# One-hot tiles of the token lists in quads of token columns

## The chip, the cores and the metric

The kernel runs on one core of a Trainium2 chip. The metric is the device time in microseconds; before the change it is 2782.22 us, the median of three runs (2782.1 to 2784.02). The engines are named as in the profile: PE is TensorE (PEld its weight loads), DVE is VectorE, ACT is ScalarE, POOL is GpSimd, SP is SyncE, which issues DMAs.

## What is computed

An attention with squared ReLU, and behind it a mixture of eight experts. Each expert takes exactly `cap` tokens; the pairs of token and expert are served in the order of their gate values. Cut to what matters:

```python
def _attn_ref(u, v, z):                       # u, v: (8, 2496, 256), z: (8, 2496, 64)
    scores = (1.0 / S) * np.matmul(z, z.transpose(0, 2, 1))
    out = np.matmul(np.maximum(scores, 0.0) ** 2, v)
    return u * out

def _moe_ref(x, w_gate, w1, w2):              # x: (19968, 256), 8 experts, F = 1024
    cap = N // E                              # 2496
    order = np.argsort(-(x @ w_gate).flatten())
    for idx in order:
        tok, e = idx // E, idx % E
        if assigned[tok] >= 0 or counts[e] >= cap:
            continue
        assigned[tok] = e
        counts[e] += 1
    for e in range(E):
        mask = assigned == e
        out[mask] = np.maximum(x[mask] @ w1[e], 0.0) @ w2[e]
    return out
```

## The kernel before

**Attention** (`attention`, up to about 1515 us) goes over 8 batches, 5 groups of 512 queries and 20 key tiles, with fp32 values split in two parts. It isn't touched.

**Tokens on the chip.** The gate values of all 19968 tokens lie as 128 partitions by J = 156 columns, padded to JP = 160. A token is a partition p and a column j; `idi` (L192 to L197) holds its number, `idh` and `idl` (L198 to L204) the number's upper part (divided by 128) and lower part (modulo 128) in bf16.

**Routing** (`route(k)`, L247) finds, eight times, the next expert that is full: a search for its threshold by histograms (L285 to L336; `hist`, L226, counts with the matmuls of L231), the tokens at the threshold (L339 to L352), which expert it is (L353 to L383), and then its list of tokens. For the list, each token of the expert gets a rank (L396 to L401). `rab` (L402 to L406) holds for each token the rank's upper part, `rab[:, 0]` (which of KT = 20 columns of the list), and its lower part, `rab[:, 1]` (which of 128 rows).

**The list** (L413 to L441) is made by matmuls, one for each token column j: the stationary operand is a one-hot tile `ob` of the row (128 slots), the moving operand `hl` holds the one-hot of the column times `idh`, and times `idl`. Summed over the 156 token columns in one PSUM tile, that puts each token's number at its place: L440 and L441 make it the integers `idx`, by which POOL gathers tokens (L450) and later writes results (L574). The columns go in four quarters of CB = 40. For each quarter DVE makes `oa` (L421: `rab[:, 0]` compared with `slot`), `hl` (L424, twice) and `ob` (L431, four pieces of 32 slots), and PE multiplies (L436). `slot` (L207) holds 0 to 127, each 40 times, and is filled by an iota on POOL. In all four tiles the 40 token columns are innermost, so that DVE's operations run along them; a matmul picks one of them, and its operands have a step of 40 elements: 128 stationary columns, and 2 x 20 = 40 moving columns. List 0 is made in two passes, of 4 and of 16 list columns (8 and 32 moving columns), which keep the same `ob` tiles.

**The experts** (L581 to L628) run in steps of (expert k, 512 tokens, 128 hidden values): `layer1` (L515, matmuls of L510 to L512, evictions L529 on ACT and L530 on DVE), `layer2` (L545, L541 to L543), transposes of gathered tokens (`turn_x`, L498 to L503), weights (`load_w`, L453, gathers on POOL; `split_w`, L464, whose L477 runs on POOL).

**Order.** `route(0)` runs first, alone. Each later `route(k)` is a generator that `advance` (L607) carries a step further twice in each step of expert k - 1, so that its instructions stand among those of the experts on DVE and PE; all of it must be done before expert k starts. A yielded number is how much of this pace a piece takes. `behind(4)` (L244) puts the instructions that make `ob` behind the L530 of four steps ago in DVE's order. The tiles `oa` and `hl` have two buffers, `ob` has four.

Of the kernel before, what the change touches and what calls it, by code (L numbers as in the profile page):

```python
# [10 lines left out]
BF = mybir.dt.bfloat16  # L11
# [3 lines left out]
OP = mybir.AluOpType  # L15
# [6 lines left out]
def tile_attention_then_moe(ctx, tc, u, v, z, w_gate, w1, w2, out):  # L22
# [36 lines left out]

    attention(tc, u, v, z, w_gate, xd, identf, made, first, 1.0 / S)  # L60
    moe(tc, xd, first, jp, identf, w1, w2, out, B, S, consts)


# [32 lines left out]
def moe(tc, xd, first, jp, identf, w1, w2, out, B, S, cp):  # L96
    nc = tc.nc
# [3 lines left out]
    KT = NT + 1  # L101
# [18 lines left out]
    with ExitStack() as ctx:  # L120
        rp = ctx.enter_context(tc.tile_pool(name="rp", bufs=1))
# [4 lines left out]
        def const(shape, dt, name):  # L126
            return cp.tile(shape, dt, name=name)
# [59 lines left out]
        for c in range(2):  # L187
            for h in range(DH):
# [6 lines left out]
                       base=0, channel_multiplier=NT)  # L195
# [8 lines left out]
        nc.vector.tensor_copy(idl, idh_i)  # L204

        CB = JP // 4
        slot = rp.tile([128, 128, CB], BF, name="slot")  # L207
        nc.gpsimd.iota(slot, pattern=[[1, 128], [0, CB]], base=0, channel_multiplier=0,  # L208
                       allow_small_or_imprecise_dtypes=True)

        asg = const([128, JP], BF, "asg")
        nc.vector.memset(asg, 0.0)
# [7 lines left out]
        def srch():  # L220
            return ps.tile([128, 512], F32, name="srch")
# [22 lines left out]
        def behind(lag):  # L244
            return tc.issue_after(paced[-lag].ins) if len(paced) >= lag else nullcontext()

        def route(k):  # L247
# [29 lines left out]
            else:  # L277
# [7 lines left out]
                for stage in range(2):  # L285
                    V = floor
                    for r, w in enumerate(widths):
                        n = (1 << w) - 1
# [6 lines left out]
                        for h in range(nh):  # L295
                            t = rp.tile([128, JP // nh, n], BF, name=f"mask{h}")
                            for a in range(0, n, 8):
                                z = min(8, n - a)
# [17 lines left out]
                        p = srch()  # L316
# [11 lines left out]
                    if stage == 0:  # L328
                        base = rp.tile([128, 1], F32, name="base")
# [16 lines left out]
                p = srch()  # L346
# [40 lines left out]
            p = srch()  # L387
# [14 lines left out]
            rab = rp.tile([128, 2, JP], BF, name="rab")  # L402
# [10 lines left out]
            obs = {}  # L413
            for a0, a1 in ((0, 4), (4, KT)) if k == 0 and KT > 4 else ((0, KT),):
                na = a1 - a0
                p = srch()
                for c in range(0, JP, CB):
                    q = slice(c, c + CB)
                    oa = rp.tile([128, KT, CB], BF, name="oa", bufs=2)[:, :na]
                    hl = rp.tile([128, 2, KT, CB], BF, name="hl", bufs=2)[:, :, :na]  # L420
                    nc.vector.tensor_tensor(oa, rab[:, 0, None, q].to_broadcast([128, na, CB]), slot[:, a0:a1],  # L421
                                            op=OP.is_equal)
                    for i, d in enumerate((idh, idl)):
                        nc.vector.tensor_mul(hl[:, i], oa, d[:, None, q].to_broadcast([128, na, CB]))  # L424
                    yield 1.5
                    if a0 == 0:
                        obs[c] = rp.tile([128, 128, CB], BF, name="ob", bufs=4)
                        for b in range(0, 128, 32):
                            z = b + 32
                            with behind(4):  # L430
                                nc.vector.tensor_tensor(obs[c][:, b:z],  # L431
                                                        rab[:, 1, None, q].to_broadcast([128, z - b, CB]),
                                                        slot[:, b:z], op=OP.is_equal)
                            yield 1.5
                    for j in range(c, min(J, c + CB)):
                        nc.tensor.matmul(p[:, :2 * na], obs[c][:, :, j - c], hl[:, :, :, j - c],  # L436
                                         start=(j == 0), stop=(j == J - 1))
                    yield
                idl_f = rp.tile([128, KT], F32, name="idl_f")[:, :na]
                nc.vector.tensor_copy(idl_f, p[:, na:2 * na])  # L440
                nc.vector.scalar_tensor_tensor(idx[:, a0:a1], p[:, :na], 128.0, idl_f, op0=OP.mult, op1=OP.add)  # L441
# [158 lines left out]
        for _ in route(0):  # L600
            pass
        N = len(seq)
        done = 0
        steps_k = {k: 0 for k in range(E)}
        gens = {k: route(k) for k in range(1, E)}

        def advance(pos):  # L607
# [340 lines left out]
```

## Time and profile before

| | |
|---|---|
| median of three runs | 2782.22 us (2782.1 to 2784.02) |
| span of the profiled execution, on its one core | 2781.9 us |
| mean granted clock of TensorE | 0.957 |
| attention | to about 1515 us |
| routing of the first expert, alone | about 1515 to 1614 us |
| experts, with the routing of the next | about 1615 to 2575 us |
| last expert | 2575 us to the end |
| list matmuls L436 | 1404: 156 with 8 moving columns, 156 with 32, 1092 with 40 |
| `ob` on DVE, L431 | 128, mean 847 ns |
| `oa` on DVE, L421, with 800 elements | 28, mean 1344 ns |
| iota of `slot` on POOL, L208 | 1, 5062 ns |

The span runs from the first to the last instruction of one profiled execution; it lies 0.3 us below the median of the runs. A row of the timeline gives the start and the duration in us, engine, line, operation, `out<-in`, shape, how many instructions are merged (x40), and in brackets how long the engine was idle before and what ended that. A row of the groups gives `busy us, mean ns | idle before, releaser`. A row of the windows gives a stretch, its length, the busy time (and instructions) of PE, PEld, DVE, ACT and POOL, then the granted clock of TensorE as a share of full speed, the busy share of the DMA engines and their GB/s; where the window is limited to one line, only the engines of this line stand there. Matmuls overlap, so the time that one takes in a stream is the distance of starts, not its duration.

### The profile page before, as it was taken

To read this page: it belongs to the slowest core of one execution; us is meant where nothing else is said; L and a number is where in the kernel's file an instruction comes from. 1 tells how busy PE (TensorE), PEld (TensorE's weight loads), DVE (VectorE), ACT (ScalarE), POOL (GpSimd) and SP (SyncE) were. 2 spreads that over 40 slices of the span, in tenths; PEclk is the share of its full clock that TensorE was granted. 3 is DMA by queue.
4 is the path that set the end of the run, shared out by engine and by line. 5 is a ranking of instruction groups with operands and counts; after the bars stand their busy time and mean duration, and the time that the engine had idled before them with its cause. 6 is when DMAs were issued, how large, how long until landed. Compare 5 with 4: busy or idle time off the path is not lost.

```text
span 2781.9 us, 51744 instructions
## 1 busy us (share of the span) xinstructions
PE 2671.3 (96%) x19733; PEld 2501.6 (90%) x19733; DVE 1996.2 (72%) x6053; ACT 1651.1 (59%) x2851; POOL 495.9 (18%) x608
## 2 busy tenths in 40 slices
PE   9999999999999999999998489999999999999998
PEld 8999999999999999999998378888888898988998
DVE  7787887787888877878877777676666767676222
ACT  8898888888888988888886022322223222323232
POOL 2000000000000000000000342434343334335341
PEclk9999999999999999999999588999999898989999
DMA  4120221210212202102000011111111111112110
GB/s 135 44 74 26 60 68 33 65 61 24 82 38 60 68 31 58 53 31 66 31 24 15 28 47 47 51 55 40 58 45 62 35 43 60 37 63 66 41 45 26
DMA packets 49417, 138.88 MB, mean 50 GB/s; under 512 B 10896, under 2 KB 18576, under 8 KB 48272
## 3 DMA queue, kind: packets, MB, share of 16 engines
q1 hardware_dynamic: 29200, 77.88, 9.2%
q0 software_dynamic: 19968, 57.70, 6.4%
q8 instruction: 154, 2.52, 0.4%
q14 instruction: 95, 0.78, 0.1%
HBM read 85.47 MB, written 40.89 MB: 45 GB/s over the span
## 4 chain that ended last, share of the span: by engine, by line
PE 89%; DVE 6%; issue 3%; POOL 1%; DMA 1%; ACT 0%; POOLq 0%; ACTq 0%; SPq 0%
PE acc L787 14%; PE acc L784 14%; PE acc L786 13%; PE sc L744 7%; PE sc L743 7%; PE y L541 5%; PE hp L510 5%; PE y L542 5%; PE y L543 5%; PE hp L511 5%; PE hp L512 4%; PE srch L436 3%; PE srch L231 2%; PE xp L498 1%; DVE oa L421 1%
## 5 line engine op out<-in xcount | busy, mean ns | idle before, releaser
L787 PE MATMUL acc<-vl,hi 128*128 128x256 f32 x3200 | 896.9, 282 | 0.0
L784 PE MATMUL acc<-vh,hi 128*128 128x256 f32 x3200 | 893.6, 281 | 0.0
L786 PE MATMUL acc<-vh,lo 128*128 128x256 f32 x3040 | 853.9, 281 | 0.0
L768 DVE TENSOR_TENSOR lo<-a,hi 128x512 fp32r<-128x512 f32 (+1 forms) x760 | 518.7, 683 | 222.2 <-ACT hi L757 207.8
L784 PEld LDWEIGHTS acc<-vh,hi 128*128 128x128 f32 x3200 | 602.1, 188 | 28.7
L787 PEld LDWEIGHTS acc<-vl,hi 128*128 128x128 f32 x3200 | 602.1, 188 | 1.7
L786 PEld LDWEIGHTS acc<-vh,lo 128*128 128x128 f32 x3040 | 571.5, 188 | 31.1
L529 ACT ACTIVATE hh<-hp 128x512 fp32r<-128x512 f32 (+1 forms) x320 | 187.1, 587 | 645.6 <-PE hp L512 575.0
L746 ACT ACTIVATE r<-sc 128x512 f32<-128x512 f32 (+1 forms) x800 | 468.8, 586 | 142.6 <-PE sc L744 137.6
L751 ACT ACTIVATE a<-r 128x512 f32<-128x512 f32 (+1 forms) x800 | 496.9, 621 | 24.4
L814 DVE SCALAR_TENSOR_TENSOR lt<-xs,wgb 128x256 bf16<-128x256 f32 x1248 | 480.0, 431 | 0.3
L541 PE MATMUL y<-w2h,hh 128*128 128x256 f32 (+1 forms) x1280 | 375.1, 293 | 0.0
L542 PE MATMUL y<-w2l,hh 128*128 128x256 f32 (+1 forms) x1280 | 369.9, 289 | 0.0
L743 PE MATMUL sc<-za 128*128 128x512 f32 (+1 forms) x800 | 316.9, 396 | 0.0
L744 PE MATMUL sc<-zb,za 128*128 128x512 f32 (+1 forms) x800 | 313.5, 392 | 0.0
L757 ACT ACTIVATE hi<-a 128x512 fp32r<-128x512 f32 (+1 forms) x480 | 298.2, 621 | 14.6
L208 POOL IOTA slot<- 128x5120 bf16 x1 | 5.1, 5062 | 1485.5 <-DVE xs L797 1485.5
L510 PE MATMUL hp<-xh,w1h 128*128 128x512 f32 (+2 forms) x646 | 269.4, 418 | 0.0
L541 PEld LDWEIGHTS y<-w2h,hh 128*128 128x128 f32 (+1 forms) x1280 | 249.9, 195 | 11.2 <-ACT hh L529 0.4
L542 PEld LDWEIGHTS y<-w2l,hh 128*128 128x128 f32 (+1 forms) x1280 | 249.5, 195 | 9.4
L511 PE MATMUL hp<-xl,w1h 128*128 128x512 f32 (+2 forms) x646 | 257.3, 398 | 0.0
L512 PE MATMUL hp<-xh,w1l 128*128 128x512 f32 (+2 forms) x646 | 255.2, 395 | 0.0
(1142 smaller groups left out, 3918.8 us busy)
## 6 DMA issues: line engine op xcount, KB each, us to landing
vr<-in_v_dram SPq DMA_DIRECT2D x32, 512.0 KB, 3.7
ur<-in_u_dram SPq DMA_DIRECT2D x32, 512.0 KB, 4.4
xd<-xs SPq DMA_DIRECT2D x32, 512.0 KB, 2.9
zb<-za SPq DMA_DIRECT2D x14, 640.0 KB, 6.7
zin<-in_z_dram SPq DMA_DIRECT2D x32, 128.0 KB, 2.1
vr<-in_v_dram SPq DMA_DIRECT2D x8, 384.0 KB, 3.2
ur<-in_u_dram SPq DMA_DIRECT2D x8, 384.0 KB, 4.5
xd<-xs SPq DMA_DIRECT2D x8, 384.0 KB, 2.3
```

What stands on the lines that cost most here:

```text
L510: nc.tensor.matmul(p[:, c], wh, xh, start=(d == 0), stop=False)
L541: nc.tensor.matmul(o, h[:, c], wh, start=first, stop=False, skip_group_check=True)
L542: nc.tensor.matmul(o, h[:, c], wl, start=False, stop=False, skip_group_check=True)
L743: nc.tensor.matmul(p, k, ZA[b][:, q], start=True, stop=False)
L744: nc.tensor.matmul(p, k, ZB[b][:, q], start=False, stop=True)
L746: nc.scalar.activation(r, p, AF.Relu, scale=scale)
L751: nc.scalar.activation(a, R.pop(n), AF.Square)
L768: nc.vector.tensor_sub(l, a, h.bitcast(F32))
L784: nc.tensor.matmul(o, h[:, c], vh, start=(kt == 0 and i % 2 == 0), stop=False, skip_group_check=True)
L786: nc.tensor.matmul(o, l[:, c], vh, start=False, stop=False, skip_group_check=True)
L787: nc.tensor.matmul(o, h[:, c], vl, start=False, stop=last, skip_group_check=True)
L814: nc.vector.scalar_tensor_tensor(t[r], XS[b, g][r, i], 1.0, WG["rows"][r, e], op0=OP.mult, op1=OP.mult, accum_out=lg[r, j, e:e + 1])
```

## The change

The 40 token columns of a quarter are cut into QN = 10 quads of QW = 4. In `oa`, `hl` and `ob` the quad comes first and the 4 columns of a quad are innermost: `[10, 20, 4]`, `[10, 2, 20, 4]` and `[10, 128, 4]` in place of `[20, 40]`, `[2, 20, 40]` and `[128, 40]`. The tiles keep their sizes. `slot` holds each number 4 times, 512 elements in place of 5120, and is read again for each quad; rows of `rab`, `idh` and `idl` are read through `by_quad`, 4 at a time, again for each slot. A matmul picks quad n and column r in it; its operands have a step of 4 elements (8 bytes) in place of 40 (80 bytes).

```diff
         CB = JP // 4
-        slot = rp.tile([128, 128, CB], BF, name="slot")
-        nc.gpsimd.iota(slot, pattern=[[1, 128], [0, CB]], base=0, channel_multiplier=0,
+        QW = 4
+        QN = CB // QW
+        slot = rp.tile([128, 128, QW], BF, name="slot")
+        nc.gpsimd.iota(slot, pattern=[[1, 128], [0, QW]], base=0, channel_multiplier=0,
                        allow_small_or_imprecise_dtypes=True)
+
+        def by_quad(row, n):
+            return row.rearrange("p (q r) -> p q r", r=QW)[:, :, None, :].to_broadcast([128, QN, n, QW])
...
-                    oa = rp.tile([128, KT, CB], BF, name="oa", bufs=2)[:, :na]
-                    hl = rp.tile([128, 2, KT, CB], BF, name="hl", bufs=2)[:, :, :na]
-                    nc.vector.tensor_tensor(oa, rab[:, 0, None, q].to_broadcast([128, na, CB]), slot[:, a0:a1],
-                                            op=OP.is_equal)
+                    oa = rp.tile([128, QN, KT, QW], BF, name="oa", bufs=2)[:, :, :na]
+                    hl = rp.tile([128, QN, 2, KT, QW], BF, name="hl", bufs=2)[:, :, :, :na]
+                    nc.vector.tensor_tensor(oa, by_quad(rab[:, 0, q], na),
+                                            slot[:, None, a0:a1].to_broadcast([128, QN, na, QW]), op=OP.is_equal)
                     for i, d in enumerate((idh, idl)):
-                        nc.vector.tensor_mul(hl[:, i], oa, d[:, None, q].to_broadcast([128, na, CB]))
+                        nc.vector.tensor_mul(hl[:, :, i], oa, by_quad(d[:, q], na))
...
-                        obs[c] = rp.tile([128, 128, CB], BF, name="ob", bufs=4)
+                        obs[c] = rp.tile([128, QN, 128, QW], BF, name="ob", bufs=4)
...
-                                nc.vector.tensor_tensor(obs[c][:, b:z],
-                                                        rab[:, 1, None, q].to_broadcast([128, z - b, CB]),
-                                                        slot[:, b:z], op=OP.is_equal)
+                                nc.vector.tensor_tensor(obs[c][:, :, b:z], by_quad(rab[:, 1, q], z - b),
+                                                        slot[:, None, b:z].to_broadcast([128, QN, z - b, QW]),
+                                                        op=OP.is_equal)
...
                     for j in range(c, min(J, c + CB)):
-                        nc.tensor.matmul(p[:, :2 * na], obs[c][:, :, j - c], hl[:, :, :, j - c],
+                        n, r = divmod(j - c, QW)
+                        nc.tensor.matmul(p[:, :2 * na], obs[c][:, n, :, r], hl[:, n, :, :, r],
                                          start=(j == 0), stop=(j == J - 1))
```

No instruction is added, removed or moved: on each engine the instructions stand in the same order as before, and only the shapes of the lines in the diff differ.

## The prediction

> **What bounds the kernel now.** I read the busy times first, then the chain of work that ended last, then the stretch in which the changed lines run.
>
> ```profile
> PE 2671.3 (96%) x19733; PEld 2501.6 (90%) x19733; DVE 1996.2 (72%) x6053; ACT 1651.1 (59%) x2851; POOL 495.9 (18%) x608
> PE 89%; DVE 6%; issue 3%; POOL 1%; DMA 1%; ACT 0%; POOLq 0%; ACTq 0%; SPq 0%
> PE acc L787 14%; PE acc L784 14%; PE acc L786 13%; PE sc L744 7%; PE sc L743 7%; PE y L541 5%; PE hp L510 5%; PE y L542 5%; PE y L543 5%; PE hp L511 5%; PE hp L512 4%; PE srch L436 3%; PE srch L231 2%; PE xp L498 1%; DVE oa L421 1%
> 1621.00:2575.00 954.00, 914.99 (x6716) 831.66 (x6716) 656.60 (x1649) 268.96 (x434) 366.81 (x333) 0.93 0.16 50
> ```
>
> TensorE (PE) is the bound: 96% busy and 89% of the chain. The list matmuls, L436, hold 3% of it. The last row is the stretch in which experts run while the next one's list is made: PE 915.0 of 954 us, VectorE (DVE) 656.6, ScalarE (ACT) 269.0, GpSimd (POOL) 366.8, granted clock 0.93. PE time saved there shortens the span unless DVE becomes late.
>
> **The list matmuls.** For each expert after the first (k from 1 to 7) 156 of them run in bursts. This is PE's timeline around the bursts of k = 1 (start, duration, count, idle before), with the clock over two of them from the windows view, limited to that line, and the group by shape:
>
> ```profile
> 1704.00 3.66 PE L436 MATMUL srch<-hl,ob 128*128 128x40 bf16 x40 [0.98 <-DVE ob L431]
> 1707.44 0.77 PE L510 MATMUL hp<-xh,w1h 128*128 128x512 f32 x1
> ...
> 1721.61 3.66 PE L436 MATMUL srch<-hl,ob 128*128 128x40 bf16 x40
> 1725.05 0.48 PE L510 MATMUL hp<-xh,w1h 128*128 128x512 f32 x1
> ...
> 1731.38 0.40 PE L512 MATMUL hp<-xh,w1l 128*128 128x512 f32 x1
> 1731.62 6.78 PE L436 MATMUL srch<-hl,ob 128*128 128x40 bf16 x76
> 1738.17 0.56 PE L541 MATMUL y<-w2h,hh 128*128 128x256 f32 x1
> 1704.00:1707.40 3.40, 3.40 (x40) 3.40 (x40) 0.50 0.00 0
> 1721.70:1725.00 3.30, 3.30 (x40) 3.30 (x40) 1.00 0.00 0
> L436 PE MATMUL srch<-hl,ob 128*128 128x40 bf16 x1092 | 98.8, 273 | 2.5 <-DVE ob L431 2.5
> ```
>
> From a burst's start to the next matmul's start are 3.44, 3.44 and 6.55 us, 86 ns for each list matmul. It is the same at a granted clock of 0.50 and of 1.00, so the array is not the limit; reading the operands is. The L512 row streams 512 fp32 columns in 0.24 us (to the next start), 0.47 ns a column; 40 columns at 86 ns are 2.15 ns each. Next the counts at the threshold (L231), whose weights have no step and whose 32 moving columns come in two runs of 16, and then the list matmuls of list 0, with 8 and with 32 columns, and a window over them.
>
> ```profile
> 1680.34 0.42 PE L231 MATMUL srch<-fmask,oh 128*128 128x32 bf16 x10
> 1680.61 0.48 PE L512 MATMUL hp<-xh,w1l 128*128 128x512 f32 x1
> ...
> 1577.38 2.64 PE L436 MATMUL srch<-hl,ob 128*128 128x8 bf16 x40 [6.01 <-DVE ob L431]
> ...
> L436 PE MATMUL srch<-hl,ob 128*128 128x8 bf16 x156 | 10.3, 206 | 8.3 <-DVE ob L431 8.3
> 1573.00:1594.00 21.00, 13.20 (x201) 12.85 (x202) 18.09 (x44) 2.38 (x2) 19.75 (x6) 0.50 0.20 59
> ...
> 1608.68 5.01 PE L436 MATMUL srch<-hl,ob 128*128 128x32 bf16 x76
> 1613.51 1.51 PE L498 MATMUL y<-identf,xg 128*128 128x128 f32 x6
> ```
>
> Ten counts take 0.27 us, 27 ns each. In list 0, with only 8 moving columns, 40 list matmuls take 2.64 us; less the 0.21 us of the last one, over 39, that is 62 ns. Eight columns at 2.15 ns would be 17, so it is the weights, read at a step of 40, that take 62 (at a granted clock of 0.50). With 32 columns it is (1613.51 - 1608.68) / 76 = 64 ns. I read this as two streams side by side, of which the slower one counts: the weights with 62 ns, 40 moving columns with 86.
>
> **What a step of 4 costs.** No row shows one. The bounds are 86 ns (any step costs the same) and 27 ns (a step of 4 costs nothing). A step of 4 bf16 elements is 8 bytes, next to the 4-byte step of the fp32 row at 0.47 ns a column, and far from 80 bytes. I take 30 ns. Saved for k from 1 to 7: 1092 x (86 - 30) = 61.2 us (0 to 64.4).
>
> [...]
>
> In list 0 the first 156 wait for DVE (0.76 us and more per burst) and what they feed waits for POOL:
>
> ```profile
> 1590.47 0.15 DVE L441 SCALAR_TENSOR_TENSOR idx<-srch,idl_f 128x4 int32<-128x4 f32 x1
> ...
> 1605.35 1.03 POOL L450 DMA_INDIRECT xg<-xd,idx  x1 [0.16 <-issue]
> ```
>
> The indices are there 14.9 us before POOL's first gather, so nothing is gained. The last 76 stand ahead of transposes on PE: 76 x (64 - 30) = 2.5 us (0 to 2.8).
>
> **The clock.** Windows right behind the second burst and behind the long one, of k = 1 and of k = 6, and behind the second burst of k = 7; the third last column is the granted clock:
>
> ```profile
> 1725.05:1731.62 6.57, 6.57 (x32) 5.44 (x30) 5.04 (x9) 1.14 (x2) 0.00 (x0) 0.74 0.01 2
> 1738.17:1745.62 7.45, 7.45 (x38) 6.86 (x37) 4.87 (x17) 0.60 (x1) 4.52 (x5) 0.67 0.22 59
> ...
> 2482.32:2487.36 5.04, 5.04 (x31) 4.09 (x30) 4.47 (x8) 1.14 (x2) 0.00 (x0) 1.00 0.00 0
> 2493.91:2501.36 7.45, 7.45 (x42) 7.04 (x41) 5.48 (x18) 0.75 (x2) 4.53 (x5) 0.77 0.20 55
> 2545.00:2548.00 3.00, 3.00 (x14) 2.81 (x14) 0.71 (x2) 0.60 (x1) 0.00 (x0) 0.53 0.00 0
> ```
>
> The clock falls though PE is never idle: a burst that mostly waits for its reads counts as little work. Duration times (1 - clock) is what the dense matmuls behind it lose: 1.7 and 2.5 us for k = 1. Over the 12 windows of k = 1 to 6 (clocks 0.74, 0.74, 0.74, 0.76, 0.77, 1.00 behind the second burst, 0.67 to 0.77 behind the long one) and the one of k = 7 the sum is 21.8 us. With 30 ns the bursts last 1.2 and 2.3 us and do more per time. I take 20 us (0 to 21.8), since a shorter burst may still cost the clock here and there. The low clock at the first burst (0.50 above) comes from a stall that stays (below). That it ends sooner behind a burst that is 2.2 us shorter is worth at most half of that, 1.1 us, or 6 us for six k; I count nothing.
>
> **DVE.** The one-hot operations keep their counts and elements; their inner rows become 4 long. L421 and L431 give the rate now; L70 re-reads a row of 8, L71 reads rows of 4 out of 8, L74 repeats one element along its row:
>
> ```profile
> 1573.84 0.24 DVE L421 TENSOR_TENSOR oa<-rab,slot 128x160 bf16<-128x160 bf16 x1
> ...
> 1728.49 0.81 DVE L431 TENSOR_TENSOR ob<-rab,slot 128x1280 bf16<-128x1280 bf16 x1
> ...
> L74 DVE TENSOR_TENSOR oh<-code,code8b 128x320 bf16<-128x320 bf16 x28 | 13.7, 489 | 0.7
> L70 DVE TENSOR_TENSOR eq<-eq,code8b 128x320 bf16<-128x320 bf16 x28 | 9.1, 324 | 0.5
> L71 DVE TENSOR_TENSOR eq<-eq 128x160 bf16<-128x160 bf16 x28 | 6.6, 235 | 0.2
> ...
> 1701.20 0.38 PE L543 MATMUL y<-w2h,hl__24588 128*128 128x256 f32 x1 [3.92 <-DVE hl__24588 L530]
> ```
>
> (0.81 - 0.24) / 1120 is 0.51 ns an element, plus 0.16 us. By that L70 would take 0.32 us and L71 0.24, and they do, so short rows and rows read again keep the rate; L74 comes to 1.03. I take 0.51, a cost of nothing. At 1.03 an L431 takes 0.67 us more. Before the first burst of each k PE already waits for DVE (3.92 us in the last row, then 0.98 at the burst), so there four L431 and an L424 would add 3.1 us, 22 us for seven k, and half of the 12 us that sixteen of them add in list 0: 28 us. That stall itself stays, since it lies ahead of the burst. At the long burst DVE is ahead: its last L431 ends at 1729.3, PE comes at 1731.62. If the 1.7 us of low clock in between go, 0.6 of this cover is left, and any more is a wait of that length.
>
> **The iota of slot**, on POOL, has 512 elements in place of 5120. It lies at the start of routing, where PE waits:
>
> ```profile
> 1516.04 5.06 POOL L208 IOTA slot<- 128x5120 bf16 x1 [1485.50 <-DVE xs L797]
> 1517.09 1.95 PE L831 MATMUL misc<-wgt,xt 128*128 128x8 f32 x16 [0.47 <-ACT xt L828]
> 1517.67 3.47 DVE L282 COPY hd<-nrow 128x15 f32<-128x15 f32 x1
> 1519.08 2.05 DVE L835 COPY lg<-misc 128x24 f32<-128x24 f32 x1
> ...
> L282 DVE COPY hd<-nrow x7: 170/170/3466, 1517.7 to 2292.8; 128x15 f32<-128x15 f32 x7
> ```
>
> L282 takes 0.17 us elsewhere and 3.47 here: it ends when the iota does. With a tenth of the elements, some 0.5 us,, the logits' copies (L835, L837) wait only for L831, which ends at 1519.04. They would be through near 1519.3, where they now are at 1521.2: 1.9 us (0 to 3.3).
>
> **Sum**: 61.2 + 2.5 + 20 + 1.9 = 85.6 us. The span of the profiled execution is 2781.9, 0.3 below the median of 2782.2. Forecast: 2697 us.
>
> **Rivals.**
> - *Half of the way.* If the price is for each stretch that a read fetches, and it holds two of the new columns, the burst runs at 86 / 2 = 43 ns: 1092 x 43 = 47 us, list 0 1.5, iota 1.9, clock 18. That is 2714.
> - *Weights stay slow.* If weights come quickly only where neighbours lie side by side, as in the 27 ns row, the 62 ns of the row with 8 columns stay and only the moving side gains: 1092 x 24 = 26 us, clock some 12, iota 1.9, so 2742. [...]
> - *The clock falls all the same*, since 43 or 30 ns is still thin work: 2717.
> - *DVE drops to 1.04 ns while PE gains*: 2697 + 28 = 2725. L70 and L71 speak against it.
> - *No change on PE*: any step costs 86 ns. Only the iota is left: 2780. Against it stands the fp32 row.
> - *Slower.* DVE drops to 1.04 ns in the L431 ahead of each first burst (+28 us) and PE stays at 86 ns: 2808. It decides as long as a list matmul takes more than 86 - (28 - 1.9) / 1.092 = 62 ns; below that PE's gain is the larger one.
>
> **How the numbers follow.** Chances: forecast 0.45, half 0.20, weights 0.10, clock 0.08, DVE with gain 0.07, no change 0.06, slower 0.04. The lower end takes all bounds (64.4 + 2.8 + 21.8 + 3.3 + 6 = 98): 2684. The upper end takes in all but the last two, 1 in 10: 2744. A measurement of this kernel tells about 0.2% (5.6 us) from no change: faster 0.90, same 0.06, slower 0.04.
>
> **What would show it.** The next start behind 40 list matmuls comes after 1.2 us, not 3.44, and after 76 after 2.3, not 6.55; at 1.7 us the half rival is right, at 2.5 the weights one. The windows behind them show a clock near 1.00. L431 stays at 0.82 us, and L282 takes 0.17. I am wrong if the interval is under 40 ns and the span hardly moves: then PE waits elsewhere, most likely for L530 behind the one-hot operations.

## The result and the profile after

The changed kernel takes 2705.08 us, the median of four runs (2703.23 to 2707.3), beside 2783.12 (2782.1 to 2786.07) for four runs of the kernel before: a ratio of 0.9724, with an interval of 0.9712 to 0.9735. The forecast was 2697. The span of the profiled execution went from 2781.9 to 2705.5 us, by 76.4. In the changed kernel's profile the lines from the diff on stand five or six higher: the list matmuls are L442 (were L436), `ob` is L436 (L431), the experts' matmuls are L516 to L518 and L547 to L549. First the page's busy times and the head of its chain:

```profile
PE 2585.9 (96%) x19733; PEld 2419.7 (89%) x19733; DVE 1998.9 (74%) x6053; ACT 1650.7 (61%) x2851; POOL 497.7 (18%) x608
PE 89%; DVE 7%; issue 2%; DMA 1%; POOL 1%; ACT 0%; POOLq 0%; ACTq 0%
```

The instructions are the same in number, and PE is 85.4 us less busy (2671.3 before) with DVE 2.7 us more. PE is still the bound, with 89% of the chain as before. Its timeline around the bursts of k = 1, as shown of before, with the row of the stall ahead of the first burst:

```profile
1697.18 0.39 PE L549 MATMUL y<-w2h,hl__24588 128*128 128x256 f32 x1 [3.92 <-DVE hl__24588 L536]
...
1699.99 1.83 PE L442 MATMUL srch<-hl,ob 128*128 128x40 bf16 x40 [1.26 <-DVE ob L436]
1701.65 0.78 PE L516 MATMUL hp<-xh,w1h 128*128 128x512 f32 x1
...
1715.26 1.80 PE L442 MATMUL srch<-hl,ob 128*128 128x40 bf16 x40
1716.90 0.47 PE L516 MATMUL hp<-xh,w1h 128*128 128x512 f32 x1
...
1721.92 3.28 PE L442 MATMUL srch<-hl,ob 128*128 128x40 bf16 x76
1725.03 0.37 PE L547 MATMUL y<-w2h,hh 128*128 128x256 f32 x1
```

From a burst's start to the next row are 1.66, 1.64 and 3.11 us (before 3.44, 3.44 and 6.55): 41 ns for a list matmul, where there were 86. The stall of 3.92 us ahead of the first burst is as it was. Next the windows behind the three bursts:

```profile
1701.65:1714.64 12.99, 12.99 (x78) 11.64 (x74) 10.91 (x19) 3.59 (x6) 4.46 (x4) 0.86 0.10 42
1716.90:1721.92 5.02, 5.02 (x33) 4.07 (x29) 4.45 (x8) 1.14 (x2) 0.00 (x0) 1.00 0.01 3
1725.03:1732.50 7.47, 7.47 (x56) 7.10 (x53) 6.97 (x22) 1.15 (x2) 4.59 (x5) 1.00 0.20 56
```

Behind the second burst and the long one the clock is 1.00 (it was 0.74 and 0.67); it is so for every k. Behind the first burst, which follows the stall, it is 0.86, where the same stretch of before has 0.83. The ledger needs one window more of each kernel, from the first list burst of k = 1 to the first of k = 7. Before:

```profile
1704.00:2525.94 821.94, 787.93 (x5749) 717.69 (x5750) 565.07 (x1417) 232.08 (x374) 314.56 (x285) 0.92 0.15 49
```

and after:

```profile
1699.99:2458.14 758.15, 721.60 (x5749) 654.43 (x5749) 568.90 (x1417) 231.79 (x374) 319.67 (x285) 0.97 0.16 53
```

Both hold the same 5749 matmuls, 936 of them list matmuls (six k of 156). The stretch is 63.8 us shorter. The list matmuls give 936 x (86 - 41) = 42.1 us of it. PE's busy time fell by 66.3, so the other matmuls, the same as before, took 24.2 us less: that is the clock, 0.92 against 0.97. PE's idle time grew from 34.0 to 36.6 us, which takes 2.5 back (below). Ahead of the stretch 4.0 us went (1704.00 to 1699.99), behind it 8.6, of which 156 x 45 ns = 7.0 are the list matmuls of k = 7.

The 4.0 us ahead are list 0 and the iota. List 0 (32 moving columns, the last 76 matmuls):

```profile
1575.36 1.49 PE L442 MATMUL srch<-hl,ob 128*128 128x8 bf16 x40 [6.01 <-DVE ob L436]
...
1606.74 2.73 PE L442 MATMUL srch<-hl,ob 128*128 128x32 bf16 x76
1609.31 0.58 PE L504 MATMUL y<-identf,xg 128*128 128x128 f32 x2
...
L442 PE MATMUL srch<-hl,ob 128*128 128x8 bf16 x156 | 5.8, 175 | 11.7 <-DVE ob L436 11.7
```

The 76 take 2.57 us instead of 4.83, 34 ns each. With 8 moving columns it is (1.49 - 0.175) / 39 = 34 ns too, 62 before. The iota and what it held, in the timeline:

```profile
1515.92 1.21 POOL L210 IOTA slot<- 128x512 bf16 x1 [1485.36 <-DVE xs L803]
1516.97 1.95 PE L837 MATMUL misc<-wgt,xt 128*128 128x8 f32 x16 [0.47 <-ACT xt L834]
1517.56 0.17 DVE L287 COPY hd<-nrow 128x15 f32<-128x15 f32 x1
1518.96 0.18 DVE L841 COPY lg<-misc 128x24 f32<-128x24 f32 x1 [1.24 <-PE misc L837]
1519.40 0.69 PE L236 MATMUL srch<-mask,oh 128*128 128x240 bf16 x5 [0.48 <-DVE lg L843]
```

L287 takes 0.17 us (3.47 before, as L282), and the logits' copy follows its matmuls. The gate matmul L837 starts at 1516.97, 2.43 us ahead of the first count; in the kernel before these are 1517.09 and 1521.41, 4.32 us. So 1.9 us went here.

The idle time that was added lies ahead of the first bursts, where PE waits for `ob`. The group row of before, in the prediction, has 2.5 us of such waits; here it is

```profile
L442 PE MATMUL srch<-hl,ob 128*128 128x40 bf16 x1092 | 48.6, 214 | 5.3 <-DVE ob L436 5.3
```

At k = 1 the burst starts 2.80 us after the end of the stall in the kernel before (1701.20 to 1704.00) and 2.81 us after it here (1697.18 to 1699.99): DVE's last `ob` sets that time. PE's ten matmuls in between got faster, so PE waits 1.26 us in place of 0.98. At k = 2 the same ten take 2.02 us at a clock of 0.65, 2.50 before at 0.50, and the wait is 0.78 in place of 0.30. So 2.5 us of what the clock gave did not shorten the span.

PE also waits in the searches, and there nothing was added: 11.2 us in this stretch before, 10.1 after. But what it waits for changed. At k = 1 it was L238 before (PE idle for 1.48 us):

```profile
1755.53 3.03 POOL L477 TENSOR_TENSOR w1l<-wr,w1h 128x512 fp32r<-128x512 f32 x2
1756.66 1.98 DVE L238 TENSOR_TENSOR hx<-hr,dE 128x56 fp32r<-128x56 f32 x1
```

and it is the mask behind L298 now (PE idle for 1.48 us again):

```profile
1742.59 3.03 POOL L483 TENSOR_TENSOR w1l<-wr,w1h 128x512 fp32r<-128x512 f32 x2
1743.12 2.53 DVE L298 TENSOR_TENSOR T<-next,Dg 128x7 int16<-128x7 f32 x1
```

L238 takes 0.22 us elsewhere (on average in the kernel after, as L243), and L298 a median of 0.17. Both end here within 0.1 us of the end of the same POOL subtraction (L477, now L483). In five of the k it holds L238 before, and L298 after.

### The profile page after: what moved, and what is told of

Same layout as the page of the kernel before. It is cut to its first block, busy times and chain, and to the rows that moved or that the text cites. A ratio compares the mean times of both kernels' runs of the same rounds, so it can differ in the third digit from the quotient of the medians.

```text
span 2705.5 us, 51744 instructions
## 1 busy us (share of the span) xinstructions
PE 2585.9 (96%) x19733; PEld 2419.7 (89%) x19733; DVE 1998.9 (74%) x6053; ACT 1650.7 (61%) x2851; POOL 497.7 (18%) x608
## 4 chain that ended last, share of the span: by engine, by line
PE 89%; DVE 7%; issue 2%; DMA 1%; POOL 1%; ACT 0%; POOLq 0%; ACTq 0%
PE acc L793 14%; PE acc L790 14%; PE acc L792 13%; PE sc L750 7%; PE sc L749 7%; PE hp L516 5%; PE y L547 5%; PE y L549 5%; PE y L548 5%; PE hp L517 5%; PE hp L518 5%; PE srch L442 2%; PE srch L236 2%; PE xp L504 1%; DVE ob L436 1%
## 5 line engine op out<-in xcount | busy, mean ns | idle before, releaser
L547 PE MATMUL y<-w2h,hh 128*128 128x256 f32 (+1 forms) x1280 | 367.9, 288 | 0.0
L548 PE MATMUL y<-w2l,hh 128*128 128x256 f32 (+1 forms) x1280 | 363.3, 284 | 0.0
L763 ACT ACTIVATE hi<-a 128x512 fp32r<-128x512 f32 (+1 forms) x480 | 298.2, 621 | 14.6
L516 PE MATMUL hp<-xh,w1h 128*128 128x512 f32 (+2 forms) x646 | 264.7, 411 | 0.1
L518 PE MATMUL hp<-xh,w1l 128*128 128x512 f32 (+2 forms) x646 | 252.2, 390 | 0.0
L547 PEld LDWEIGHTS y<-w2h,hh 128*128 128x128 f32 (+1 forms) x1280 | 242.3, 189 | 10.9 <-ACT hh L535 0.4
L548 PEld LDWEIGHTS y<-w2l,hh 128*128 128x128 f32 (+1 forms) x1280 | 242.4, 189 | 9.1
```

The source lines that it names most:

```text
L516: nc.tensor.matmul(p[:, c], wh, xh, start=(d == 0), stop=False)
L547: nc.tensor.matmul(o, h[:, c], wh, start=first, stop=False, skip_group_check=True)
L548: nc.tensor.matmul(o, h[:, c], wl, start=False, stop=False, skip_group_check=True)
```

## Experiments

The kernels ran on chips where the kernel before takes 2811.74 us (first four kernels), 2813.12 (the next four) and 2812.22 (the last two), some 29 us more than beside the result. Why was not tried; the change itself (`a_quads`) is longer there by as much between its first list burst of k = 1 and its last list matmul, 827 us against 798. The times in the expectations of the first four kernels count from the result's chip (2782 us before, 2705 with quads), so only their differences can be compared. Each is compared with the runs of before that stand beside it, or with `a_quads`, the change itself on such a chip. The list matmuls are L445 in all kernels but `a_quads`, `ob` is L439. `QO` stands for the group width of `ob`, `QH` for that of `oa` and `hl`; 40 is the old layout.

**One operand alone.** Which stream sets the interval, and do the two add up?

```diff
-        QW = 4
+        QO, QH = 4, 40
...
-                        n, r = divmod(j - c, QW)
-                        nc.tensor.matmul(p[:, :2 * na], obs[c][:, n, :, r], hl[:, n, :, :, r],
+                        n, r = divmod(j - c, QO)
+                        n2, r2 = divmod(j - c, QH)
+                        nc.tensor.matmul(p[:, :2 * na], obs[c][:, n, :, r], hl[:, n2, :, :, r2],
```

> Only ob (the stationary operand) is laid out in quads; oa and hl keep their 40 columns in a row, so the moving operand has its step of 40 again. Theory (two streams side by side, the slower one counts): the 40 moving columns set 86 ns per list matmul as before, and 34 ns with the 8 moving columns of list 0, where the weights count; the clock falls behind the bursts as before; about 2778 us, that is the old time less the iota and little else. Rival (both reads share one path and add up): half of the columns read come cheaper, an interval near 60 ns, and about 2735 us.

The other kernel has `QO, QH = 40, 4`. Both keep an iota of 5120 elements beside that of 512.

> Only oa and hl are in quads; the stationary operand ob has its step of 40 again. Theory (the slower stream counts): the weights set 62 ns per list matmul, with 8 as with 40 moving columns, so the bursts take 2.5 and 4.8 us; 1092 x (86 - 62) = 26 us from the interval, and some of the clock behind the second burst; 2735 to 2750 us. Rival (the reads add up): an interval nearer to 75 ns and about 2765 us.

The second burst of k = 1 in PE's timeline, the first burst of list 0, and the window behind the former, with the weights alone in quads:

```profile
1724.37 3.62 PE L445 MATMUL srch<-hl,ob 128*128 128x40 bf16 x40
1727.78 0.48 PE L519 MATMUL hp<-xh,w1h 128*128 128x512 f32 x1
...
1576.59 1.50 PE L445 MATMUL srch<-hl,ob 128*128 128x8 bf16 x40 [6.01 <-DVE ob L439]
...
1727.78:1732.78 5.00, 5.00 (x25) 4.41 (x22) 3.96 (x7) 0.60 (x1) 0.00 (x0) 0.66 0.02 3
```

and with the moving columns alone in quads:

```profile
1725.03 2.65 PE L445 MATMUL srch<-hl,ob 128*128 128x40 bf16 x40
1727.52 0.48 PE L519 MATMUL hp<-xh,w1h 128*128 128x512 f32 x1
...
1577.24 2.64 PE L445 MATMUL srch<-hl,ob 128*128 128x8 bf16 x40 [6.01 <-DVE ob L439]
...
1727.52:1732.55 5.03, 5.03 (x31) 4.08 (x30) 4.45 (x8) 1.15 (x2) 0.00 (x0) 1.00 0.01 3
1737.28:1742.28 5.00, 5.00 (x29) 4.73 (x28) 3.54 (x13) 0.60 (x1) 2.73 (x3) 0.74 0.13 34
```

With the weights alone the interval stays at 85 ns (3.41 / 40) and the time too: 2812.95 us, a ratio of 1.0005 (0.9996 to 1.0015). Yet with 8 moving columns the burst takes 1.50 us, 34 ns a matmul: the weights have become quick, and the moving columns hide it. With the columns alone it is 62 ns (2.49 / 40), the old price of the weights: 2775.79 us, 0.9869 (0.9852 to 0.9885), 36 us less than before, where the theory had 32 to 47. So in these two runs two streams run side by side and the slower one counts; they don't add up. Here the clock behind the second burst is 1.00, behind the long one 0.74 at k = 1, 0.50 at k = 2 and 3, and 1.00 at k = 4 to 6.

**Another width.** What does a step cost, from 80 bytes to 4?

```diff
-        QW = 4
+        QO, QH = 2, 2
```

> Groups of 2 token columns in place of 4, for all tiles: a step of 4 bytes. If a read pays for each separate stretch of memory and a step of 8 bytes shares it between two columns, a step of 4 bytes shares it between four: interval 27 to 30 ns, as in the histogram counts, 1092 x (41 - 28) = 14 us less than the quads, 2690 us, provided that DVE keeps 0.51 ns an element (L431 at 0.82 us). Rival: the interval is at its floor with quads and stays at 41 ns, 2705 us. Second rival: DVE loses speed on rows of 2 (L431 at 1.3 to 1.5 us), the gain on PE goes into the wait ahead of the first burst of each expert: 2705 to 2720 us.

```diff
-        QW = 4
+        QO, QH = 8, 8
```

> Groups of 8 token columns for all tiles: a step of 16 bytes. If one read brings in 16 bytes and each separate one has its price, no two columns share one and the interval is back at 86 ns, 2775 us. If the price grows with the step, it lies between: 50 to 70 ns, 2720 to 2750 us. If the stretch is longer than 16 bytes, it stays at 41 ns and 2705 us.

`e3b_pairs` is the same kernel beside the change itself:

> The change as it is, timed beside the other kernels of this group on one chip: 41 ns per list matmul, 0.972 of the kernel before.

> Groups of 2 token columns again, beside the quads on one chip. The interval went from 41 to 26 ns at the full clock: 1092 x 15 = 16 us less than the quads if PE's time still goes to the span; nothing if DVE has become late behind it. L439 as long as with quads (0.82 us).

PE's timeline of `e3b_pairs`, second burst of k = 1:

```profile
1716.99 1.19 PE L445 MATMUL srch<-hl,ob 128*128 128x40 bf16 x40
1718.02 0.48 PE L519 MATMUL hp<-xh,w1h 128*128 128x512 f32 x1
```

and of `e4_eights`, the second burst, with the window behind it:

```profile
1720.74 3.35 PE L445 MATMUL srch<-hl,ob 128*128 128x40 bf16 x40
1723.89 0.77 PE L519 MATMUL hp<-xh,w1h 128*128 128x512 f32 x1
...
1723.89:1728.89 5.00, 5.00 (x25) 4.21 (x23) 3.22 (x5) 0.60 (x1) 0.00 (x0) 0.67 0.01 3
```

Pairs take 26 ns (1.03 / 40; the same in the long burst), eights 79 (3.15 / 40); the clock falls behind a burst of eights (0.67 behind the second of k = 1) as it did before. Times: pairs 2724.75 us, 0.9690 (0.9674 to 0.9706), and 2725.49, 0.9688 (0.9675 to 0.9702); eights 2799.88, 0.9953 (0.9936 to 0.9969); the change itself 2740.68, 0.9751 (0.9738 to 0.9765). So pairs gain another 15.2 us on quads and beat both kernels.

**The weights' own price at 8 bytes.**

```diff
-        QW = 4
+        QO, QH = 4, 2
```

> ob in quads, oa and hl in pairs: stationary operand at a step of 8 bytes, moving operand at 4. Theory (two streams, the slower one counts; in list 0 the weights alone took 34 ns with quads): the 40 moving columns no longer set 41 ns, the weights set 32 to 34 at either clock, 1092 x 8 = 9 us less than the quads. Rival (the weights set the 41 ns at the full clock, or both reads add up): 41, or halfway to 26 ns.

The second burst of k = 1:

```profile
1714.14 1.51 PE L445 MATMUL srch<-hl,ob 128*128 128x40 bf16 x40
1715.49 0.47 PE L519 MATMUL hp<-xh,w1h 128*128 128x512 f32 x1
```

34 ns (1.35 / 40, and the same at the first burst, where the clock is 0.50): with the columns in pairs the weights in quads are the slower stream, at the 34 ns that list 0 showed. 2733.04 us, 0.9722 (0.9705 to 0.9738); the quads have 0.9751, so some 8 us are gained on them, where 9 were expected.

With the moving columns side by side (`QO, QH = 4, 1`) it should stay at 34 ns:

> ob in quads, and in oa and hl the token column outermost, so that the 40 moving columns lie side by side; DVE's oa and hl then repeat one element along a row. Theory: weights alone, again 32 to 34 ns per list matmul, the same as with pairs in hl; oa and hl take 0.98 us each in place of 0.57 (1.03 ns an element), 1.3 us per quarter, of which the part ahead of the first burst of each expert shows as wait: 3 to 9 us more than with pairs in hl.

It does, but the time is 2780.87 us, 0.9890 (0.9874 to 0.9907), far from what was expected. The longest of PE's waits (us, times, longest):

```profile
PE srch L240 <- DVE mask L309: 38.4, 20, 4.4
```

DVE's operations on `oa` and `hl` got longer (0.98 us, as the expectation has it), the stall ahead of each first burst went from 3.9 to 4.8 us, and PE waits 38.4 us for masks (17.1 in `e6_cols_pairs`). But the third and fourth bursts also no longer stand together on PE, so the order of instructions changed as well. The interval is settled by this run; the 48 us to `e6_cols_pairs` are not.

**Length or thinness of a burst.** Does the clock stay because the bursts are short, or because they do more per time? Each list matmul of k from 1 to 7 runs twice, the second time into columns of the PSUM tile that nothing reads:

```diff
                                          start=(j == 0), stop=(j == J - 1))
+                        if k:
+                            nc.tensor.matmul(p[:, 256:256 + 2 * na], obs[c][:, n, :, r], hl[:, n2, :, :, r2],
+                                             start=False, stop=(j == J - 1), skip_group_check=True)
```

> Quads, and for each expert after the first every list matmul is run twice, the second time into unused columns of the same PSUM tile: bursts of 3.3, 3.3 and 6.2 us at 41 ns, as long as those before the change but with twice the work per time. Theory (thin work lowers the clock, not the length): the clock stays at 1.00 behind the bursts, and the time is that of the quads plus 1092 x 41 ns = 45 us. Rival (a burst of list matmuls of that length lowers the clock): 0.5 to 0.7 behind them as before, and 60 to 70 us more than the quads.

Windows of this kernel over the long burst of k = 1 and behind it:

```profile
1727.16:1733.41 6.25, 6.25 (x153) 6.25 (x153) 4.56 (x13) 0.60 (x1) 0.00 (x0) 1.00 0.01 4
1733.41:1738.41 5.00, 5.00 (x39) 4.70 (x36) 4.55 (x16) 0.60 (x1) 2.98 (x3) 1.00 0.19 54
```

A burst of 6.25 us at 41 ns leaves the clock at 1.00, and so do the second and the long burst of every k from 1 to 6; one of 3.4 us at 85 ns took it to 0.66 (`e1_rows_only`). So length alone does not lower it: in these runs it fell behind bursts that did less per time (62 to 86 ns a matmul). For such bursts the length still counted (62 ns in `e2_cols_only`: none lost behind 2.5 us, up to half behind 4.7), and so does something that stays open: in the kernel before, three of the four bursts of k = 7, of 3.1 to 3.4 us at 86 ns, left the clock at 1.00, and one took it to 0.66. The time is 2797.5 us, 0.9947 (0.9932 to 0.9962), 56.8 more than quads: 1092 x 41 ns = 45 are the matmuls themselves, and PE's wait for `hx`, the histogram's sums, is 14.2 us longer (28.8 against 14.6 in `a_quads`), for a reason that was not looked for.

**The iota.** A second iota of 5120 elements into a tile that nothing reads:

```diff
+        wide = rp.tile([128, 128, CB], BF, name="wide")
+        nc.gpsimd.iota(wide, pattern=[[1, 128], [0, CB]], base=0, channel_multiplier=0,
+                       allow_small_or_imprecise_dtypes=True)
```

> Quads, with a second iota of 5120 elements behind the short one, into a tile that nobody reads. Theory: L282's copy (here a few lines later) takes 3 us or more again and ends with the iota, and routing starts 1.8 to 3 us later; the rest is as with quads. Rival: the copy was slow for another reason and takes 0.17 us, no difference.

```profile
1515.07 1.98 PE L844 MATMUL misc<-wgt,xt 128*128 128x8 f32 x16 [0.47 <-ACT xt L841]
1515.17 5.05 POOL L215 IOTA wide<- 128x5120 bf16 x1
1515.65 4.62 DVE L295 COPY hd<-nrow 128x15 f32<-128x15 f32 x1
1517.09 3.18 DVE L848 COPY lg<-misc 128x24 f32<-128x24 f32 x1
...
1520.54 1.18 PE L244 MATMUL srch<-mask,oh 128*128 128x240 bf16 x5 [3.50 <-DVE lg L850]
```

The timeline shows two DVE copies of 15 and 24 elements that end with the iota, at 1520.2 to 1520.3. From the gate matmul to the first count are 5.47 us, 3.0 more than the 2.43 of `a_quads`. In the time, 2743.82 us, 0.9754 (0.974 to 0.9769), that is 3.1 us more than quads, less than the intervals can tell; the trace shows it, the time alone doesn't.

## Why the prediction was nearly right

**The step that failed is "I take 30 ns"**, and with it the term 1092 x (86 - 30) = 61.2 us. The prediction put 8 bytes "next to the 4-byte step of the fp32 row", far from 80, and so took 30 ns. A list matmul takes 41 ns, half as much again as without a step (27 ns), so the term is 49.1 us, 12.1 less. The table sets the runs side by side; the moving side has 40 columns, and the weights' own price shows where few or quick moving columns leave it bare:

| step | 40 moving columns | weights |
|---|---|---|
| 80 bytes | 86 ns | 62 ns |
| 16 bytes | 79 ns | 61 ns |
| 8 bytes | 41 ns | 34 ns |
| 4 bytes | 26 ns or less | 26 ns or less |

The 61 ns are from list 0 of `e4_eights`, whose 8-column bursts of 40 take 2.60 us, and one matmul 0.205: (2.60 - 0.205) / 39. At 4 bytes both streams fit into the 26 ns of the pairs.

From 80 to 16 bytes hardly anything is gained (86 to 79 ns), from 16 to 8 half (to 41), from 8 to 4 another third (to 26). That fits the price that the rival *half of the way* named, one for each stretch fetched, of which two new columns share one: 43 ns were worked out there, 41 came. No run shows the stretch itself; an estimate from the table is that it has 16 bytes and costs some 2 ns on the moving side (79 / 40) and 0.5 on that of the weights (61 / 128). At 4 bytes four columns would share one, which would be 20 ns; the 26 that came may be another limit, since pairs, unlike quads (41 ns at 0.50 and at 1.00), follow the clock: at the first burst of k = 1, where it is 0.50, they take 34 ns (1.35 / 40). The counts of L231, which have no step, take 27, so 26 may simply be what a matmul this small costs. That eights still take 7 ns less than the old layout, the price by stretch does not explain.

**The rest of the sum.** That the slower of two streams counts was read rightly from 86, 62 and 64 ns; `e1_rows_only` and `e2_cols_only` show it. List 0 gave 2.3 us (2.5 forecast), the iota 1.9 (1.9), DVE's one-hot operations cost nothing:

```profile
1571.97 0.82 DVE L436 TENSOR_TENSOR ob<-rab,slot 128x1280 bf16<-128x1280 bf16 x1
```

It was 0.81 to 0.82 before. The clock gave 24.2 us in the six k of the ledger against 20 in all: its mechanism was right, and `e7_twice` speaks for the reason given (1.00 behind 6.25 us at 41 ns). Of these, 2.5 us came back as PE's wait for `ob`, which stood in no step; 21.7 are left. The window behind the first burst went from 0.83 to 0.86, the part that the prediction bounded by 6 us and counted as nothing.

In sum: -12.1 for the list matmuls, -0.2 for list 0, -2.5 for the wait, +4.2 for the clock in the six k, and +1.4 that no window splits, which is 9.2 less than the 85.6 forecast: 76.4.

**The rivals.** *Half of the way* had the size of the interval and, with 18 us for the clock, 2714, which the result beat by 9, mostly by the clock. *Weights stay slow* falls: they went from 62 to 34 ns with the step alone. *The clock falls all the same* falls with the windows at 1.00. *DVE drops* and *slower* fall with L436 at 0.82 us, *no change on PE* with the interval. The point of the prediction "under 40 ns and the span hardly moves" did not come up.

## What to carry to other kernels

In these runs the times of a bf16 operand of PE that is read with a step fit a price for each 16-byte stretch that it touches (estimated from the table: 2 ns on the moving side, 0.5 on the weights), and only the slower side counts (85 ns in `e1_rows_only`, 62 in `e2_cols_only`): lay out so that both fall together, and go down to neighbours in pairs where the engine that writes the tile keeps its rate, as DVE did here with rows of 2 (`hl` 0.57 us in `e3b_pairs`, as with quads) but not of 1 (0.98 in `e5_cols_flat`). Bursts of matmuls that mostly wait for operands can cost twice, in themselves and in the clock behind them (42.1 and 24.2 us in the six k of the ledger). A faster PE gains nothing where another engine sets the next start, as `ob` does ahead of each first burst (PE's waits there went from 2.5 to 5.3 us). When a rate between two measured steps is unknown, give the prediction the price by stretch, not the nearest row; here this rival (43 ns, where 41 came) had a chance of 0.20, and the nearest row (30 ns) 0.45.

## What was not expected of the hardware

- Sixteen bytes between the elements cost nearly as much as eighty: 79 ns against 86.
- POOL's timing reaches DVE in more places than the start of routing. With the iota it is shown by `e8_wide_iota` (0.17 us, or 4.62); with the subtractions of L477 (now L483) it is only seen: L238 or L298 end with them. The stall of 3.92 us ahead of the first burst, and with it the low clock there, which the prediction took as given, looks like the same thing. These rows of the kernel before stand right ahead of it:

```profile
1691.55 4.10 DVE L421 TENSOR_TENSOR oa<-rab,slot 128x800 bf16<-128x800 bf16 x1
1692.15 3.06 POOL L477 TENSOR_TENSOR w1l<-wr,w1h 128x512 fp32r<-128x512 f32 x2
1696.18 3.14 DVE L424 TENSOR_TENSOR hl<-oa,idh 128x800 bf16<-128x800 bf16 x1
1696.52 2.37 POOL L477 TENSOR_TENSOR w2l<-wr,w2h 128x1024 fp32r<-128x1024 f32 x1
```

  The same `oa` takes 0.57 us at 1703.86, beside no such subtraction, and the second `hl` 0.56. So DVE loses some 6 us just before the L530 that PE waits for, at this place of each k from 1 to 6, and the change leaves that as it is (4.07 and 3.14 us at k = 1). No run moved the subtractions; it would be the next thing to try.
- PE with no idle time lost a third to a half of its granted clock in the 5 us behind 3.4 and 6.5 us of thin matmuls at 85 ns (`e1_rows_only`, 0.66 and 0.50 at k = 1; not behind every such burst: in the kernel before it stayed at 1.00 behind the second of k = 6), but none behind 6.25 us at 41 ns; at 62 ns it was 1.00 behind 2.5 us, and 0.50 to 1.00 behind 4.7 (`e2_cols_only`).
